# Zeroing of buffers taken off GpSimd and given to VectorE and ScalarE, with the instruction order planned anew

## The chip, the cores and the metric

The kernel runs on one core of one Trainium2 chip. The metric is device time in microseconds (us) of one execution; each kernel is executed several times and the median counts. The engines of the core that matter here are TensorE (PE, matrix products into PSUM), VectorE (DVE), ScalarE (ACT), GpSimd (POOL, which here also issues all loads) and SyncE (SP, which issues the stores). Each engine works through its own queue in order; semaphores tie the queues together.

## The reference

Two steps are fused: attention within a symmetric window of 32 positions to either side, and a mixture of eight low-rank adapters of which each token uses two. Cut to what matters:

```python
# q, k, v: (8, 8, 576, 64) float32
scores = (1 / np.sqrt(64)) * np.matmul(q, k.transpose(0, 1, 3, 2))
mask = np.abs(pos[:, None] - pos[None, :]) <= 32
scores = np.where(mask, scores, -1e9)
attn = softmax(scores, axis=-1)
x = (attn @ v).transpose(0, 2, 1, 3).reshape(4608, 512)
...
logits = x @ w_gate                      # w_gate: (512, 8)
topk = the 2 largest logits of each row
w = softmax over these two
delta = sum over the two of w * ((x @ A[e]) @ B[e])   # A[e]: (512, 16), B[e]: (16, 512)
return x + delta
```

## The kernel before

**Tiling.** The eight batches are worked one behind another in a pipeline. Two heads are worked as a pair, so a batch has four pairs; a pair is a unit u (32 in all). Of a batch, q and k each come in three tiles of 96 partitions (LD, line 275), cast from float32 to float16 by the transfer; v comes in two halves (LV, line 280) of one load for four heads each. All loads stand in GpSimd's queue, in one order; the compiled program lets eight of them be in flight, the next waits for the landing of the one eight places before it. There are seven raw buffers `l` for q and for k, three buffers `vbd` for v, two `qT` and two `kT`, four `PT`.

**Steps of the attention.** RG (line 290) regroups a raw tile on VectorE into `c`, called a cast below, three buffers deep. TR (298) transposes it on TensorE into PSUM (two slots T). EQ (304) and EK (312, two instructions, one for each half of the partitions) copy it on ScalarE into `qT` and `kT`. SV (285) moves the odd positions of a v half to other partitions on VectorE. SC (318 and 324) makes a tile of masked scores of eight key blocks in PSUM (three slots W); EX (329) takes the exponential on ScalarE into `PT`; there are 36 such tiles, 4.5 for a batch. PV (342) multiplies with v, and a column of ones in `vbd` gives the sum; MU (351 and 352) is the normalisation on VectorE, one for each unit, into `x`.

**Steps of the adapters, once for each batch.** TX (364) transposes `x`, XE (370) copies it out of PSUM on VectorE, PZ (378) makes logits and low-rank products, G1, GA and G2 (395 to 416) find the two adapters and their weights, TZ and ZE (423, 427) transpose the result, PD (433 and 436) adds x and delta in PSUM, OB (445 on ScalarE, 447 on VectorE) copies it out, ST (453) stores it from SyncE.

**What must be zeroed or set to one.** `kT` holds two heads block-diagonally, so 64x64 corners must be zero; `vbd` holds two heads side by side, so the other head's columns must be zero and one column must be one; the margins of `PT` and of `qT` must be zero. These places are written once and never overwritten. Before, VectorE did it for buffer 0 of each kind and for all four `PT`, ahead of everything else (lines 476 to 489 by way of 500 to 505). GpSimd did it for `vbd` 1, `kT` and `qT` 1 and `vbd` 2 at three fixed places in its load queue: behind the eighth and the tenth load, and behind the sixteenth, after the six transfers of the weights (491 to 497, called from 516 to 518).

**What sets the order.** `tasks()` lists all steps with an engine, a cost in us, what they depend on, and a due time: the unit they belong to plus an offset for each kind from `OFF`. `plan()` is a list scheduler: at each step it takes, for the engine that can start something earliest, the startable step with the earliest due time, and appends it to the order; it keeps count of PSUM slots and of one transfer stream. The instructions are then issued in that order, so each engine's queue follows it. The zeroing was not among the steps; the start times of the engines in `plan()` stood for it.

## Time and profile before

| | before |
|---|---|
| median of 3 runs | 161.4 us (160.46 to 161.6) |
| profiled execution | 158.86 us |
| its span, first to last instruction | 156.9 us |
| TensorE busy | 123.2 us (79%) |
| VectorE busy | 119.8 us (76%) |
| ScalarE busy | 113.1 us (72%) |
| GpSimd busy | 67.1 us (43%) |
| mean granted TensorE clock | 0.954 |

"Span" is from the first to the last instruction of the profiled execution; the execution's own time is a little longer. A row of a timeline gives the start, the duration, the engine, the line of the kernel, the operation with its output and input, and in brackets how long the engine had been idle before and what it waited for. Rows of one line that follow each other are merged (x4), and their duration is then from the first start to the last end. Rows of groups give the count, the total busy time and the mean duration of one in ns. A load on GpSimd's timeline is the time that GpSimd takes to issue it, not the transfer.

### The profile page before, as it was taken

Reading aid. Unit: us, or ns where it says so; the run is one execution under the profiler, and the core shown is the slowest. Engines: PE = TensorE matmul, PEld = TensorE weight load, DVE = VectorE, ACT = ScalarE, POOL = GpSimd, SP = SyncE. Lnnn points to the kernel's source line nnn. Section 1 sums busy time; section 2 is a strip of 40 time slices with the busy share of each in tenths; the row PEclk is TensorE's granted clock in tenths of the full one; section 3 lists DMA queues with packets and bytes.
Section 4 is the critical chain, followed back from the end, with each engine's and each line's share of the span. In section 5 each row is a group of like instructions: output and inputs, shape, how many; then the busy total and the mean of one; then the engine's idle time right before and its main releaser. Section 6 shows DMA issues by size and latency. Waiting matters only on the chain.

```text
span 156.9 us, 4220 instructions
## 1 busy us (share of the span) xinstructions
PE 123.2 (79%) x1720; PEld 103.7 (66%) x1720; DVE 119.8 (76%) x273; ACT 113.1 (72%) x141; POOL 67.1 (43%) x91
## 2 busy tenths in 40 slices
PE   0024998659988998998699989979999899893480
PEld 0013767449967896797579778967798689672250
DVE  6799928996798879996976989779688967955310
ACT  0306799944499999969898998897998992743150
POOL 7999999899848555354553407000000000000000
PEclk9999999975899999999999999999999999999659
DMA  2999569938999999999999999992420350077125
GB/s 31 150 172 113 85 97 174 122 31 115 157 188 202 190 242 203 178 260 209 183 207 234 276 200 204 142 253 63 164 87 4 106 192 7 6 280 263 61 87 214
DMA packets 38771, 24.13 MB, mean 154 GB/s; under 512 B 24800, under 2 KB 34144, under 8 KB 38752
## 3 DMA queue, kind: packets, MB, share of 16 engines
q0 software_dynamic: 33504, 14.43, 80.5%
q1 hardware_dynamic: 5248, 9.44, 17.4%
q8 instruction: 13, 0.21, 0.6%
q14 instruction: 6, 0.05, 0.1%
HBM read 28.85 MB, written 9.44 MB: 244 GB/s over the span
## 4 chain that ended last, share of the span: by engine, by line
PE 39%; DVE 18%; POOL 16%; DMA 10%; ACT 7%; issue 7%; SPq 0%; POOLq 0%; ACTq 0%; DVEq 0%
PE W L342 6%; PE W L324 5%; PE W L318 5%; DVE x L352 5%; PE W L433 5%; POOL l L275 5%; PE W L436 5%; PE T L364 4%; DMA vbd<-in_v_dram 4%; PE T L298 4%; DMA l<-in_k_dram 3%; POOL vbd L482 3%; DVE zs L416 3%; ACT kT L312 2%; PE W L378 2%
## 5 line engine op out<-in xcount | busy, mean ns | idle before, releaser
L329 ACT ACTIVATE PT<-W 128x1024 f16<-128x1024 f32 x36 | 36.2, 1028 | 6.7 <-PE W L324 6.1
L312 ACT COPY kT<-T 64x768 f16<-64x768 f16 x48 | 38.1, 794 | 3.2 <-PE T L298 2.7
L298 PE MATMUL T<-ident,c 96*128 96x96 f16 x384 | 25.1, 216 | 17.5 <-DVE c L290 15.9
L298 PEld LDWEIGHTS <-c 96*128 96x128 f16 x384 | 20.8, 104 | 18.6 <-DVE c L290 16.8
L290 DVE COPY c<-l 96x1024 f16<-96x1024 f16 x48 | 30.4, 654 | 2.1 <-DMA l<-in_q_dram 1.3
L342 PE MATMUL W<-vbd,PT 128*128 128x130 f16 x416 | 29.9, 225 | 0.8 <-ACT PT L329 0.6
L352 DVE TENSOR_TENSOR x<-W,rc 128x640 f16<-128x640 f32 x32 | 26.4, 824 | 1.2
L342 PEld LDWEIGHTS <-PT 128*128 128x128 f16 x416 | 26.4, 100 | 1.3 <-issue 1.3
L304 ACT COPY qT<-T 128x768 f16<-128x768 f16 x24 | 19.1, 800 | 10.8 <-PE T L298 10.6
L324 PEld LDWEIGHTS <-kT 128*128 128x128 f16 x288 | 19.4, 99 | 9.5 <-issue 1.0
L324 PE MATMUL W<-qT,kT 128*128 128x128 f16 x288 | 22.4, 222 | 0.2 <-ACT kT L312 0.2
L280 POOL DMA_DIRECT2D vbd<-in_v_dram x16 | 14.0, 878 | 19.5 <-DMA vbd<-in_v_dram 7.3
L318 PE MATMUL W<-ident,mask 128*128 128x512 f16 x72 | 22.2, 391 | 0.2 <-DVE x L352 0.2
L445 ACT COPY ob<-W 128x1024 f32<-128x1024 f32 x16 | 16.2, 1015 | 6.8 <-PE W L436 4.4
L370 DVE COPY xT<-T 128x1024 f16<-128x1024 f16 (+1 forms) x24 | 13.7, 598 | 8.2 <-PE T L364 7.8
L275 POOL DMA_DIRECT2D l<-in_k_dram x24 | 16.4, 684 | 6.5 <-DMA l<-in_k_dram 2.8
L433 PE MATMUL W<-B_sb,zT 128*128 128x512 f16 x40 | 16.4, 410 | 3.2 <-DVE x L352 2.4
L436 PEld LDWEIGHTS <-xT 128*128 128x128 f16 x160 | 13.3, 104 | 8.3 <-issue 4.1
L275 POOL DMA_DIRECT2D l<-in_q_dram x24 | 15.7, 653 | 2.9 <-issue 1.2
L436 PE MATMUL W<-ident,xT 128*128 128x128 f16 x160 | 16.7, 231 | 0.0
L285 DVE COPY vbd<-vbd 32x2304 f16<-32x2304 f16 x16 | 13.9, 868 | 0.5
L364 PE MATMUL T<-ident,x 128*128 128x128 f16 x160 | 13.1, 231 | 0.1
(55 smaller groups left out, 121.1 us busy)
## 6 DMA issues: line engine op xcount, KB each, us to landing
out_dram<-ob SPq DMA_DIRECT2D x24, 256.0 KB, 2.5
l<-in_q_dram POOLq DMA_DIRECT2D x24, 192.0 KB, 9.3
l<-in_k_dram POOLq DMA_DIRECT2D x24, 192.0 KB, 9.5
vbd<-in_v_dram POOLq DMA_DIRECT2D x16, 288.0 KB, 9.4
out_dram<-ob SPq DMA_DIRECT2D x16, 192.0 KB, 2.8
WA_sb<-in_moe_A_dram POOLq DMA_DIRECT2D x4, 32.0 KB, 7.5
B_sb<-in_moe_B_dram POOLq DMA_DIRECT2D x1, 128.0 KB, 4.4
WA_sb<-in_moe_w_gate_dram POOLq DMA_DIRECT2D x1, 8.0 KB, 5.3
```

Of the source, the lines that this page charges most:

```text
L275: keep(nc.gpsimd.dma_start(out=raw[w][(NT3 * b + t) % NRAW], in_=src[FT * t:FT * t + FT]))
L290: keep(nc.vector.tensor_copy(out=cst[w][i % NCAST], in_=raw[w][i % NRAW].rearrange("p o (j d) -> p j o d", j=J)))
L298: keep(nc.tensor.matmul(out=tp[:, FT * slot:FT * slot + FT], lhsT=src[:, j, :], rhs=ident[0:FT, 0:FT], is_transpose=True, start=True, stop ...
L312: keep(nc.scalar.copy(out=dst.rearrange("p a (r f j) -> p a r f j", r=2, j=4), in_=kt[64 * o:64 * o + 64]))
L318: keep(nc.tensor.matmul(out=p[:, i:i + 4], lhsT=maskT, rhs=bcast(ident, 1, 4), start=True, stop=False))
L324: keep(nc.tensor.matmul(out=p[:, i], lhsT=kTs[b % 2][:, NB * n + a, :], rhs=qTs[b % 2][:, c0:c0 + 128], start=False, stop=(i % 4 == 3)))
L329: keep(nc.scalar.activation(out=PTs[T % NPT][:, :, 64:192], in_=ps("SC", T).rearrange("p (i c) -> p i c", c=128), func=AF.Exp, scale=1.0 / ...
L342: keep(nc.tensor.matmul(out=po[:, GS * g:GS * g + 2 * VD], lhsT=PTs[T % NPT][:, sl, off:off + 128], rhs=rhs[:, :, V0 - 1:V0 + D], start=(i ...
L352: keep(nc.vector.tensor_tensor(out=xs[b % NX].rearrange("p g (h n d) -> p g h n d", h=2, n=NP)[:, :, :, n], in0=pog[:, :, :, 1:VD], in1=bc ...
L364: keep(nc.tensor.matmul(out=tp[:, c0:c0 + 128], lhsT=xs[b % NX][:, g, 128 * c:128 * c + 128], rhs=ident, is_transpose=True, start=True, st ...
L433: keep(nc.tensor.matmul(out=pd[:, i], lhsT=zTs[b % 2][:, g], rhs=B_sb, start=True, stop=False))
L436: keep(nc.tensor.matmul(out=pd[:, i, 128 * c:128 * c + 128], lhsT=xTs[b % NXT][:, g, c], rhs=ident, start=False, stop=(c == 3)))
```

## The change

The zeroing becomes steps of the schedule. ZK (buffers `kT` and `qT`), ZV (`vbd`) and ZP (`PT`) get a cost and a due time like all others, and the steps that need the zeroed places depend on them. ZK and ZP, and ZV of `vbd` 0 and 2, are VectorE memsets; ZV of `vbd` 1 is done on ScalarE by copying from a small zeroed tile whose 66 columns are repeated 36 times. No memset is left on GpSimd except those of the identity and the mask. All offsets in `OFF` are new; the costs of some steps are lower (a q or k load 1.15 instead of 1.25, a v load 1.8 instead of 2.95, a store 0.5 instead of 0.75 for each part, SV 0.78 instead of 0.95) and one higher (G1 1.08 instead of 0.95); the engines' start times in `plan()` and its horizon differ. So the order of the instructions on every engine differs throughout. The order of the loads among themselves, and the place of the weights behind the sixteenth load, are the same, and no computing step is added or left out.

On VectorE the queue now begins with a memset of the small zero tile and one of a piece of `qT` 0; ZK of both buffers and the two columns of ones of `vbd` 1 follow, then the first cast. ZP of the four `PT` stand between the first four casts, ZV of `vbd` 0 and 2 between the following casts and shifts. On ScalarE the two copies of ZV stand first.

```diff
@@ -55,9 +55,10 @@
         self.take, self.give, self.lat = take, give, lat
 
 
-OFF = {"LD": -10.1, "LV": -8.3, "RG": -7.2, "TR": -11.5, "EQ": 11.0, "EK": -0.6, "SV": 23.8, "SC": -1.9,
-       "EX": 19.8, "PV": -0.9, "MU": -1.8, "TX": -16.6, "XE": -2.6, "PZ": 4.4, "G1": -3.0, "GA": 2.0,
-       "G2": 15.0, "TZ": 1.1, "ZE": -13.8, "PD": 9.7, "OB": 7.2}
+OFF = {"LD": -10.16, "LV": -7.58, "RG": -2.51, "TR": -3.5, "EQ": -0.91, "EK": 8.24, "SV": 11.71,
+       "SC": -2.02, "EX": 9.98, "PV": -0.24, "MU": -0.5, "TX": 0.38, "XE": -20.72, "PZ": 4.91,
+       "G1": -40.48, "GA": 17.51, "G2": -27.59, "TZ": -20.47, "ZE": 17.82, "PD": 10.1, "OB": -2.95,
+       "ZK": -28.38, "ZV": 29.47, "ZP": 16.04}
 
 
 def tasks(off=OFF):
@@ -69,6 +70,15 @@
         t.due = u + off[key[0]]
         t.seq = len(ts)
         ts[key] = t
+
+    for i in range(2):
+        for o in (0, 1):
+            add(("ZK", i, o), -4.0 + 8 * i, "DVE", 1.05, [])
+    for i in range(NPT):
+        add(("ZP", i), -3.0 + i, "DVE", 0.56, [])
+    for i in range(NV):
+        for o in (0, 1):
+            add(("ZV", i, o), 4 * i, "ACT" if i == 1 else "DVE", 2.2 if i == 1 else 1.2, [])
 
     def tiles_of(b):
         return range(NS * b // TB, (NS * b + NS - 1) // TB + 1)
@@ -79,10 +89,10 @@
             for t in range(NT3):
                 for w in (0, 1):
                     i = NT3 * b + t - NRAW
-                    add(("LD", b, w, t), u0 + 1.333 * t, "DMA", 1.25,
+                    add(("LD", b, w, t), u0 + 1.333 * t, "DMA", 1.15,
                         [("RG", i // NT3, w, i % NT3)], lat=2.0)
             for o in (0, 1):
-                add(("LV", b, o), u0 + o, "DMA", 2.95,
+                add(("LV", b, o), u0 + o, "DMA", 1.8,
                     [("PV", NP * (b - NV) + n) for n in range(NP)], lat=2.0)
             for t in range(NT3):
                 u = u0 + 1.333 * t
@@ -98,7 +108,7 @@
                 add(("EK", b, t), u, "ACT", 1.60, [("TR", b, 1, t)] + old,
                     give=("TR", b, 1, t))
             for o in (0, 1):
-                add(("SV", b, o), u0, "DVE", 0.95, [("LV", b, o)])
+                add(("SV", b, o), u0, "DVE", 0.78, [("LV", b, o)])
 
         for T in range(NT):
             last = TB * T + TB - 1
@@ -111,6 +121,7 @@
                     need |= {("EQ", bb, s // BT), ("EK", bb, s // BT)}
                     if s % NB != NB - 1:
                         need.add(("EQ", bb, (s + 1) // BT))
+                    need |= {("ZK", bb % 2, 0), ("ZK", bb % 2, 1)}
             u = (TB * T) / NB
             add(("SC", T), u, "PE", 0.90, list(need), take="W")
             pold = [("PV", v) for v in range(NU)
@@ -122,7 +133,9 @@
             bb = u // NP
             add(("PV", u), u, "PE", 0.80,
                 [("EX", T) for T in range(NB * u // TB, (NB * u + NB - 1) // TB + 1)]
-                + [("SV", bb, 0), ("SV", bb, 1)], take="W")
+                + [("ZP", T % NPT) for T in range(NB * u // TB, (NB * u + NB - 1) // TB + 1)]
+                + [("SV", bb, 0), ("SV", bb, 1), ("ZV", bb % NV, 0), ("ZV", bb % NV, 1)],
+                take="W")
             add(("MU", u), u, "DVE", 1.05,
                 [("PV", u)] + [("TX", bb - NX, h) for h in range(3)], give=("PV", u))
             if u % NP != NP - 1:
@@ -136,7 +149,7 @@
                     [("TX", bb, h)] + [("PD", bb - NXT, i) for i in range(3)],
                     give=("TX", bb, h))
             add(("PZ", bb), v0, "PE", 1.2, [("XE", bb, h) for h in range(3)], take="W")
-            add(("G1", bb), v0, "DVE", 0.95, [("PZ", bb)])
+            add(("G1", bb), v0, "DVE", 1.08, [("PZ", bb)])
             add(("GA", bb), v0, "ACT", 0.22, [("G1", bb)])
             add(("G2", bb), v0, "DVE", 1.95, [("GA", bb)], give=("PZ", bb))
             add(("TZ", bb), v0, "PE", 0.30, [("G2", bb)], take="T")
@@ -149,11 +162,11 @@
                     1.02 if n == 2 else 0.70, [("PD", bb, h), ("ST", k // 3, k % 3)],
                     give=("PD", bb, h))
                 off["ST"] = off["OB"]
-                add(("ST", bb, h), v0 + 0.8 * h, "DMO", 0.75 * n, [("OB", bb, h)], lat=2.0)
+                add(("ST", bb, h), v0 + 0.8 * h, "DMO", 0.5 * n, [("OB", bb, h)], lat=2.0)
     return ts
 
 
-def plan(off=OFF, horizon=0.0):
+def plan(off=OFF, horizon=0.036):
 
     ts = tasks(off)
     for t in ts.values():
@@ -164,7 +177,7 @@
         for d in t.deps:
             d.users.append(t)
     free = {e: 0.0 for e in ("PE", "ACT", "DVE", "DMA", "DMO")}
-    free["DMA"], free["DVE"], free["PE"], free["ACT"] = 1.5, 8.5, 9.0, 4.0
+    free["DMA"], free["DVE"], free["PE"], free["ACT"] = 1.5, 1.1, 4.5, 3.0
     slots = {"W": [0.0] * NW, "T": [0.0] * NTP}
     wait = {e: [t for t in ts.values() if t.eng == e and t.left == 0] for e in free}
     order, dma_free = [], 1.5
@@ -472,21 +485,29 @@
                                 base=64, channel_multiplier=-1,
                                 pattern=[[0, 2], [1, 2], [2, 32]]))
 
-    def init_kq(i, eng):
-        keep(eng.memset(kTs[i][0:64, :, 64:128], 0.0))
-        keep(eng.memset(kTs[i][64:128, :, 0:64], 0.0))
-        keep(eng.memset(qTs[i][:, 0:QP], 0.0))
-        keep(eng.memset(qTs[i][:, QP + NP * S:], 0.0))
-
-    def init_v(i, eng):
-        keep(eng.memset(vbd[i][0:64, :, VW + V0 - 2:VW + V0 + D], 0.0))
-        keep(eng.memset(vbd[i][64:128, :, V0 - 2:V0 + D], 0.0))
-        keep(eng.memset(vbd[i][0:64, :, V0 - 1:V0], 1.0))
-        keep(eng.memset(vbd[i][64:128, :, VW + V0 - 1:VW + V0], 1.0))
-
-    def init_p(i, eng):
-        keep(eng.memset(PTs[i][:, :, 0:64], 0.0))
-        keep(eng.memset(PTs[i][:, :, 192:256], 0.0))
+    zero = const.tile([128, D + 2], F16, name="zero")
+
+    def ZK(i, o):
+        keep(nc.vector.memset(kTs[i][64 * o:64 * o + 64, :, 64 - 64 * o:128 - 64 * o], 0.0))
+        if o == 0:
+            keep(nc.vector.memset(qTs[i][:, 0:QP], 0.0))
+            keep(nc.vector.memset(qTs[i][:, QP + NP * S:], 0.0))
+
+    def ZV(i, o):
+        c0 = V0 + VW * (1 - o)
+        dst = vbd[i][64 * o:64 * o + 64, :, c0 - 2:c0 + D]
+        if i == 1:
+            keep(nc.scalar.copy(out=dst, in_=bcast(zero[64 * o:64 * o + 64], 1, NS)))
+        else:
+            keep(nc.vector.memset(dst, 0.0))
+        c1 = V0 + VW * o
+        keep(nc.vector.memset(vbd[i][64 * o:64 * o + 64, :, c1 - 1:c1], 1.0))
+
+    def ZP(i):
+        keep(nc.vector.memset(PTs[i][:, :, 0:64], 0.0))
+        keep(nc.vector.memset(PTs[i][:, :, 192:256], 0.0))
+
+    do.update(ZK=ZK, ZV=ZV, ZP=ZP)
 
     def weights():
         for c in range(4):
@@ -496,26 +517,17 @@
                             in_=moe_w_gate.rearrange("(c p) e -> p c e", p=128)))
         keep(nc.gpsimd.dma_start(out=B_sb, in_=moe_B.rearrange("e r d -> (e r) d")))
 
+    keep(nc.vector.memset(zero, 0.0))
+    keep(nc.vector.memset(qTs[0][:, QP + S:QP + S + 32], 0.0))
     loads = 0
-    init_kq(0, nc.vector)
-    init_p(0, nc.vector)
-    keep(nc.vector.memset(qTs[0][:, QP + S * 1:QP + S * 1 + 32], 0.0))
-    init_v(0, nc.vector)
-    for i in range(1, NPT):
-        init_p(i, nc.vector)
     for t in order:
         do[t.key[0]](*t.key[1:])
         if t.key[0] in ("LD", "LV"):
             loads += 1
             if loads == 4:
                 constants()
-            elif loads == 8:
-                init_v(1, nc.gpsimd)
-            elif loads == 10:
-                init_kq(1, nc.gpsimd)
             elif loads == 16:
                 weights()
-                init_v(2, nc.gpsimd)
 
     for p in (small, psum, const):
         p.release()
```

## The prediction

> **What bounds the kernel now.** I read the page's slices first, to find where the engines are starved, then the timelines of GpSimd, VectorE and ScalarE over the first 45 us, and last a table by stretches for the transfer rate. The slices show two things: the transfers have a hole at the fourth to sixth slice and one at the ninth (a slice is 3.92 us), and the granted TensorE clock falls just behind the second.
>
> ```profile
> PEclk9999999975899999999999999999999999999659
> DMA  2999569938999999999999999992420350077125
> ```
>
> The GpSimd timeline shows what stands in the load queue at those places. Each row below is the first memset of a group, or the load that follows the group.
>
> ```profile
> 8.28 2.10 POOL L482 MEMSET vbd<- 64x2376 f16 x1
> ...
> 13.26 0.78 POOL L275 DMA_DIRECT2D l<-in_q_dram  x1
> ...
> 14.87 2.23 POOL L476 MEMSET kT<- 64x2304 f16 x1
> ...
> 19.63 0.63 POOL L275 DMA_DIRECT2D l<-in_q_dram  x1
> ...
> 29.75 2.12 POOL L482 MEMSET vbd<- 64x2376 f16 x1
> ...
> 34.75 0.65 POOL L275 DMA_DIRECT2D l<-in_q_dram  x1
> ```
>
> Start to start, the groups hold the queue for 13.26 - 8.28 = 5.0, 19.63 - 14.87 = 4.8 and 34.75 - 29.75 = 5.0 us, 14.8 in all. No load can be issued in that time. The stretches show the price (columns: stretch, its length, busy time of PE, weight loads, DVE, ACT and POOL, granted clock, DMA share, GB/s):
>
> ```profile
> 8.00:14.00 6.00, 1.80 (x21) 1.59 (x22) 5.96 (x9) 0.92 (x2) 5.89 (x6) 1.00 1.40 168
> 14.00:18.00 4.00, 2.96 (x27) 2.27 (x26) 3.94 (x4) 3.84 (x5) 3.92 (x4) 1.00 0.72 105
> 18.00:21.00 3.00, 3.00 (x34) 2.33 (x32) 2.79 (x3) 2.29 (x3) 2.94 (x6) 1.00 0.02 1
> 22.00:29.00 7.00, 6.18 (x98) 5.37 (x99) 4.81 (x10) 6.95 (x9) 6.50 (x8) 1.00 1.43 178
> 29.00:32.00 3.00, 1.14 (x15) 0.73 (x12) 3.00 (x1) 2.21 (x3) 2.96 (x4) 1.00 4.97 98
> 32.00:37.00 5.00, 3.70 (x45) 3.28 (x46) 4.63 (x6) 3.31 (x4) 4.92 (x7) 0.64 0.29 19
> 37.00:42.00 5.00, 5.00 (x60) 4.76 (x59) 3.28 (x8) 0.59 (x1) 5.00 (x8) 0.68 1.18 162
> 42.00:54.00 12.00, 11.03 (x165) 9.17 (x163) 10.79 (x29) 11.77 (x17) 7.33 (x10) 1.00 1.45 191
> 54.00:80.00 26.00, 23.31 (x365) 20.16 (x363) 22.27 (x59) 23.33 (x32) 12.27 (x17) 1.00 1.43 210
> 80.00:105.00 25.00, 24.11 (x371) 20.93 (x370) 19.87 (x51) 23.04 (x29) 7.70 (x12) 1.00 1.25 220
> ```
>
> Well supplied, loads move 162 to 191 GB/s. Against 178, the stretch 14 to 18 loses 4 x (1 - 105/178) = 1.6 us, 18 to 21 loses 3.0 and 32 to 37 loses 5 x (1 - 19/178) = 4.5: 9.1 us of dead stream. The stretch 29 to 32 is the weights, with their small pieces; they stay, and cost 3 us of the stream.
>
> The same memsets also slow VectorE. Its timeline in the first 40 us:
>
> ```profile
> 1.05 1.02 DVE L476 MEMSET kT<- 64x1152 uint32 x1 [1.05 <-PEq L536]
> ...
> 4.27 1.05 DVE L482 MEMSET vbd<- 64x1188 uint32 x1 [0.19 <-issue]
> ...
> 6.81 0.09 DVE L484 MEMSET vbd<- 64x36 f16 x1 [0.16 <-issue]
> ```
>
> ```profile
> 8.81 1.85 DVE L290 COPY c<-l 96x1024 f16<-96x1024 f16 x1
> ```
>
> ```profile
> 8.81 5.10 DVE L290 COPY c<-l 96x1024 f16<-96x1024 f16 x4
> ...
> 17.41 2.54 DVE L285 COPY vbd<-vbd 32x2304 f16<-32x2304 f16 x1
> ```
>
> ```profile
> 28.17 0.75 DVE L285 COPY vbd<-vbd 32x2304 f16<-32x2304 f16 x1
> 28.95 5.50 DVE L290 COPY c<-l 96x1024 f16<-96x1024 f16 x2
> ...
> 38.28 0.42 DVE L290 COPY c<-l 96x1024 f16<-96x1024 f16 x1 [1.06 <-DMA l<-in_q_dram]
> ```
>
> A cast takes 0.42 us and a half-shift of v (L285) 0.75 when GpSimd does no memset. Beside the memsets the first cast takes 1.85, the four from 8.81 take 5.10 in place of 1.7, the shift 2.54, the two from 28.95 take 5.50 in place of 0.8. That is 3.4 + 1.8 + 4.7 = 9.9 us of VectorE time, all in front of TensorE's transposes. ScalarE shows the result:
>
> ```profile
> 4.17 1.28 ACT L304 ACT_TABLE_LOAD   x1 [4.17 <-DVE qT L502]
> 11.57 0.80 ACT L304 COPY qT<-T 128x768 f16<-128x768 f16 x1 [6.12 <-PE T L298]
> ```
>
> ```profile
> 41.41 1.02 ACT L329 ACTIVATE PT<-W 128x1024 f16<-128x1024 f32 x1 [4.44 <-PE W L324]
> ```
>
> It starts its first copy at 11.57, and the eighth exponential (EX 7), which needs only the first two batches, is over only at 42.4. From 54 to 105 TensorE is busy 23.31 of 26 and 24.11 of 25 us: there it is the limit, and the loads stay ahead.
>
> **The change, part by part.** *GpSimd's memsets go.* The 14.8 us leave the load queue. The ninth load follows the eighth at once, then the loads are limited by the transfers (eight can be in flight, by the program's semaphores). The stream ends 9.1 us earlier if nothing else holds it.
>
> *VectorE's head.* In the new order twelve memsets stand before the first cast: four of 64x1152 (kT, both buffers) at 1.02 plus a 0.19 gap, and eight small ones at about 0.1. So the first cast starts at 1.05 + 4 x 1.21 + 0.8 = 6.7, not 8.81, and takes 0.42, not 1.85. From the end of the first cast before (10.66) to the first copy on ScalarE (11.57) it is 0.91 us, so this copy starts at 6.7 + 0.42 + 0.91 = 8.0. The memsets of PT and of vbd 0 and 2 stand between the casts now. What VectorE gains in work is two kT parts (2.04), two vbd parts (2.1) and seven small ones (0.6), 4.7 us; what it sheds is the 9.9 us of slowed copies. Net it is relieved in the head.
>
> *ScalarE zeroes vbd 1* by two copies of 2376 elements. No such copy is in the trace; the nearest rows are the copy of 768 elements at 0.80 and the exponential of 1024 at 1.03, 0.9 ns for each further element. My estimate is 0.80 + 1608 x 0.0009 = 2.2 us each. Behind the table load (1.28, from about 1.2, since its writer is now VectorE's first memset) they end at 7.0, and ScalarE's first real work is at 8.0, so they cost nothing. If the repeated source doubled them they would end at 11.4 and delay the first copy by 3.4.
>
> *ScalarE's chain to EX 7.*
>
> ```profile
> L329 ACT ACTIVATE PT<-W 128x1024 f16<-128x1024 f32 x36 | 36.2, 1028 | 6.7 <-PE W L324 6.1
> L312 ACT COPY kT<-T 64x768 f16<-64x768 f16 x48 | 38.1, 794 | 3.2 <-PE T L298 2.7
> ```
>
> The new order has 6 copies of q, 12 halves of k and 8 exponentials up to there: 6 x 0.80 + 12 x 0.794 + 8 x 1.028 = 22.6 us. From 8.0 the chain ends at 30.6; before it ended at 42.4: 11.8 us earlier. The loads must hold with it.
>
> ```profile
> l<-in_q_dram POOLq DMA_DIRECT2D x24, 192.0 KB, 9.3
> ...
> vbd<-in_v_dram POOLq DMA_DIRECT2D x16, 288.0 KB, 9.4
> ```
>
> A q or k tile is 0.197 MB, a v half 0.295, a batch 1.77. Batch 0 is in at about 14 (168 GB/s in 8 to 14). At 178 GB/s the seven transfers up to batch 1's last k (1.475 MB) are in at 14 + 8.3 = 22.3; ScalarE wants it at 8.0 + 5 x 0.80 + 10 x 0.794 + 5 x 1.028 = 25.1. Batch 2's first pair is in at 14 + 9.9 + 3 (weights) + 2.2 = 29.1, its second at 31.3. ScalarE itself wants the first only at 30.6, so both fit.
>
> *The order planned anew.* The new VectorE order puts the casts of a batch earlier. Batch 2's first three casts stand ahead of normalisation 4 and of the copies of batch 0's transposes, which free the PSUM for EX 7's scores; so VectorE blocks until 31.3 there, and behind that come the third cast, normalisation 4 with its reciprocal (1.0) and a copy or two (0.7 each) before those scores: EX 7 ends near 34 to 35, not 30.6. That is a gain of 8 there. Further on, the last cast of batch 4 follows normalisation 11 (before: 13), that of batch 7 follows normalisation 23 (before: 26). VectorE works in order, so a late load now holds up normalisation 12 or 24, and with it TensorE, which waits for their PSUM.
>
> ```profile
> 68.58 0.20 DVE L351 RECIPROCAL rc<-W 128x10 f32<-128x10 f32 x1
> ```
>
> ```profile
> 115.86 0.22 DVE L351 RECIPROCAL rc<-W 128x10 f32<-128x10 f32 x1 [0.57 <-PE W L342]
> ```
>
> ```profile
> q1 hardware_dynamic: 5248, 9.44, 17.4%
> ```
>
> These are normalisations 12 and 24. Shifted by 10 us they come at 58.6 and 105.9. Stores take 17.4% of 156.9 us, 3.4 us of the stream for each batch. Batch 4's last k needs 6.78 MB behind the first eight loads: at 191 GB/s 35.5 us, with weights (3) and about half a batch of stores (2) it is in at 54.5. Batch 7's last k needs 12.09 MB: 63.3 us, with weights and three batches of stores (10.2) at 90.5. So the loads keep ahead of both. For the rest of the new order, ScalarE's and TensorE's included, the trace has no price. Its bounds are the 4.6 us that TensorE idles between 42 and 105 (0.97 + 2.69 + 0.89), if a better order fills them, and as much the other way; I take zero, the middle, because the same instructions run there on the same three nearly full engines. The last batch's chain from normalisation 31 to the last store has no step less or more: zero, within 1 us.
>
> *Sum.* ScalarE's chain alone would give 11.8, the stream gives 9.1, the block at batch 2 leaves 8 at EX 7. As the loads have 4 us in hand at batch 4, part of that block can be made good (TensorE stood at half clock at this point before); I take 10, between the stream and the chain: span 156.9 - 10 = 146.9. The profiled execution took 158.86 us, 1.96 over its span, so 148.9 for such an execution. The median of the runs shown, 161.4, lies 2.54 above it; on that scale it is 151.4 us.
>
> **A rule that speaks against it.** GpSimd now issues its loads while VectorE copies at full speed.
>
> ```profile
> 47.93 1.11 POOL L275 DMA_DIRECT2D l<-in_k_dram  x1 [0.47 <-DVE c L290]
> ...
> 96.46 0.83 POOL L280 DMA_DIRECT2D vbd<-in_v_dram  x1
> ```
>
> The first issue overlaps a VectorE copy and takes 1.11 us, where one of the same kind takes 0.65 at 34.75: 0.46 more. Even if each of 64 loads paid that, 29 us would be spread over the 95 up to the last issue, in which the queue mostly waits for landings, so I price it at nothing. The Trainium skill (SBUF — State Buffer, section "SBUF: two separate sides") warns that descriptors of transfers issued from GpSimd cannot be written while VectorE runs a copy in a two-port mode. Its measured case has an issue of about 620 ns grow to about 3100; by that 64 loads would need 198 us and the kernel would be slower than before. The trace shows the direction and a fifth of the size.
>
> **The rivals.** *More gain:* the new order also fills TensorE's 4.6 us of idle time: 151.4 - 4.6 = 146.8. For it speaks that VectorE's casts stand earlier, against it that TensorE is at 96% from 80 to 105 already.
>
> *The loads become the bound:* if they run at 162 GB/s, as from 37 to 42, batch 4's last k takes 41.9 us and is in at 60.9, and normalisation 12, behind the last cast, comes at 61.3, 7.3 us earlier than before, not 10: 161.4 - 7.3 = 154.1.
>
> *Slower, through the casts that stand ahead:* VectorE blocks at batch 7's last cast, behind normalisation 23, and normalisation 24 comes later than 115.9. That takes 14 + 3 + 10.2 + L over 115.5, so L over 88.3 us for 12.09 MB, under 137 GB/s. At 130 GB/s it is 93 us, normalisation 24 at 120.6, the time 161.4 + 4.7 = 166. No stretch with a full queue is that slow.
>
> *Slower, through issues locked out by VectorE's copies:* the last load before was issued at 96.46; it would have to come after that again, so 70 issues would have to take over 1.37 us each. The row above has 1.11.
>
> *The change does little:* the memsets were hidden, and another limit holds the head. The holes in the stream and the clock of 0.64 behind them speak against it: 161.
>
> **How the numbers follow.** Forecast 0.50 (148.5 to 153); more gain 0.20 (145 to 148.5); loads bound 0.15 (153 to 158); little 0.05; the two slower ones 0.07 and 0.03. Changes under 1% cannot be told from none here; that is 159.8 to 163.0. So faster 0.85, same 0.05, slower 0.10. The range reaches from the second case's lower end to the third's upper end, 145 to 158, and leaves out the last three cases and the edges.
>
> **What would show it.** GpSimd's rows should hold loads back to back up to the weights, and the slices no hole in the transfers before 35 us; the first 12 casts should take 0.42 each, and the v shifts 0.75; ScalarE's first copy should start near 8 and EX 7 end near 34; the granted clock should not fall to 0.5 near 35. Normalisations 12 and 24 should come near 59 and 106. I am wrong if VectorE's rows show casts ended by a wait for a load, several us each, after 45 us, if a GpSimd issue takes 1.5 us or more in the middle, or if ScalarE's zeroing copies end after 8 us.

## The result and the profile after

| | before | after |
|---|---|---|
| median (lowest to highest) | 160.93 us (160.29 to 161.6) | 150.15 us (147.73 to 151.74) |
| profiled execution | 158.86 us | 148.89 us |
| its span | 156.9 us | 146.7 us |
| TensorE, VectorE, ScalarE, GpSimd busy | 123.2, 119.8, 113.1, 67.1 us | 119.8, 113.3, 116.3, 51.9 us |
| mean granted TensorE clock | 0.954 | 0.979 |

The changed kernel takes 0.9215 of the time before, with an interval of 0.9116 to 0.9315; the kernel before was run again beside it. Two later comparisons with the same two kernels gave 0.9307 [0.9247, 0.9368] and 0.9447 [0.9374, 0.9521]. That is a gain of 8.9 to 12.6 us. The ratios and their intervals leave out executions that took over 1.5% longer than the fastest of the same kernel; the medians take all. Effects of a us or two are as small as the scatter between comparisons, so each experiment below is set against the changed kernel of its own comparison where there is one.

First the slices of after, in the same two rows as before: granted clock and DMA share, 40 slices of 3.67 us.

```profile
PEclk9999999999999999999999999999999999999686
DMA  2999999999999999999999959990542023058035
```

Both holes in the transfers are gone, and the clock falls only in the tail. The table by stretches of after has the columns of the prediction's (stretch, length, PE, weight loads, DVE, ACT, POOL, granted clock, DMA share, GB/s):

```profile
8.00:14.00 6.00, 5.02 (x43) 3.70 (x44) 5.06 (x13) 5.56 (x8) 4.52 (x7) 1.00 1.40 164
14.00:18.00 4.00, 3.15 (x42) 2.40 (x41) 3.45 (x7) 3.67 (x6) 2.55 (x4) 1.00 1.30 197
18.00:21.00 3.00, 2.14 (x35) 1.73 (x33) 2.67 (x6) 2.32 (x3) 2.41 (x3) 1.00 1.54 196
...
32.00:37.00 5.00, 4.88 (x85) 4.52 (x83) 4.56 (x11) 3.94 (x5) 2.60 (x4) 1.00 1.46 174
...
54.00:80.00 26.00, 23.96 (x359) 20.46 (x357) 22.16 (x52) 22.90 (x30) 11.10 (x16) 1.00 1.36 225
80.00:105.00 25.00, 24.59 (x379) 21.39 (x377) 22.56 (x61) 23.60 (x32) 3.27 (x4) 1.00 0.87 160
```

The stretch 18 to 21 moved 1 GB/s and now moves 196; 32 to 37 moved 19 and now moves 174. TensorE, which did 1.80 us of work in the first of these stretches, does 5.02. The timeline of VectorE in after shows the casts (now line 303), the v shifts (298) and the normalisations (364):

```profile
6.43 0.42 DVE L303 COPY c<-l 96x1024 f16<-96x1024 f16 x1
...
28.71 0.42 DVE L303 COPY c<-l 96x1024 f16<-96x1024 f16 x1 [1.50 <-DMA l<-in_q_dram]
29.67 0.47 DVE L303 COPY c<-l 96x1024 f16<-96x1024 f16 x1 [0.54 <-DMA l<-in_k_dram]
...
31.12 0.47 DVE L303 COPY c<-l 96x1024 f16<-96x1024 f16 x1 [0.38 <-DMA l<-in_q_dram]
31.51 0.20 DVE L364 RECIPROCAL rc<-W 128x10 f32<-128x10 f32 x1
...
59.47 0.20 DVE L364 RECIPROCAL rc<-W 128x10 f32<-128x10 f32 x1
...
63.55 0.76 DVE L303 COPY c<-l 96x1024 f16<-96x1024 f16 x2 [0.35 <-PE T L311]
...
104.38 0.22 DVE L364 RECIPROCAL rc<-W 128x10 f32<-128x10 f32 x1 [0.67 <-PE W L355]
```

The first cast takes 0.42 us where it took 1.85. The rows at 28.71, 29.67 and 31.12 are the forecast block at batch 2: VectorE waits there for loads, and normalisation 4 (31.51) comes behind. The groups of instructions show the same over all 48 casts, and what it does to TensorE's transposes. First the groups of before (count, busy time, mean ns of one, idle time ahead of them and what ended it), then of after:

```profile
L290 DVE COPY c<-l 96x1024 f16<-96x1024 f16 x48 | 30.4, 654 | 2.1 <-DMA l<-in_q_dram 1.3 <-DMA l<-in_k_dram 0.5
...
L298 PE MATMUL T<-ident,c 96*128 96x96 f16 x384 | 25.1, 216 | 17.5 <-DVE c L290 15.9 <-ACT kT L312 1.6
```

```profile
L311 PE MATMUL T<-ident,c 96*128 96x96 f16 x384 | 24.0, 213 | 9.9 <-DVE c L303 8.0 <-ACT kT L325 0.9 <-ACT qT L317 0.3
...
L303 DVE COPY c<-l 96x1024 f16<-96x1024 f16 x48 | 20.3, 450 | 3.3 <-DMA l<-in_q_dram 2.3 <-DMA l<-in_k_dram 0.5 <-PE T L311 0.4
```

A cast takes 450 ns in the mean instead of 654, and TensorE's wait for casts ahead of its transposes falls from 15.9 to 8.0 us.

The timeline of ScalarE has the two zeroing copies, the first copy of work, and EX 7:

```profile
2.04 4.36 ACT L500 COPY vbd<-zero 64x2376 f16<-64x2376 f16 x2
7.78 0.80 ACT L317 COPY qT<-T 128x768 f16<-128x768 f16 x1 [1.38 <-PE T L311]
...
32.59 1.02 ACT L342 ACTIVATE PT<-W 128x1024 f16<-128x1024 f32 x1 [1.99 <-PE W L337]
```

The zeroing ends at 6.40, 1.38 us ahead of the first copy, as that row's wait says. Last the load queue on GpSimd's timeline:

```profile
71.81 0.82 POOL L293 DMA_DIRECT2D vbd<-in_v_dram  x1 [8.50 <-PE W L355]
...
86.47 0.82 POOL L293 DMA_DIRECT2D vbd<-in_v_dram  x1 [8.99 <-PE W L355]
...
88.63 1.11 POOL L293 DMA_DIRECT2D vbd<-in_v_dram  x1
```

The queue has become so early that it stands still for 8.5 and 9.0 us, because all three `vbd` buffers are still being read. The loads are ahead of their users, not behind.

**Where the time went.** The normalisations are one for each unit, and always in the same order; their start times measure how far the kernel has come. (Each number is the start of a reciprocal's row, as the three above; the last column is the span. c1 and c2 are the changed kernel again, in later comparisons; the numbers in brackets are those of the experiments below.)

| kernel | no. 0 | no. 4 | no. 7 | no. 12 | no. 31 | end |
|---|---|---|---|---|---|---|
| before | 24.02 | 38.62 | 50.03 | 68.58 | 136.26 | 156.9 |
| after | 19.43 | 31.51 | 40.63 | 59.47 | 127.51 | 146.7 |
| c1 | 20.64 | 32.75 | 41.68 | 60.91 | 129.08 | 148.1 |
| c2 | 19.80 | 32.33 | 41.72 | 60.82 | 129.31 | 148.5 |
| zero_moved (1) | 23.05 | 36.42 | 47.16 | 65.49 | 133.20 | 154.3 |
| order_only (2) | 23.53 | 41.47 | 51.05 | 69.12 | 137.66 | 157.0 |
| weights_later (3) | 19.51 | 29.33 | 39.78 | 59.59 | 126.94 | 146.0 |
| zero_placed (4) | 26.81 | 36.79 | 47.28 | 66.18 | 133.90 | 154.8 |
| old_lengths (5) | 19.97 | 31.44 | 40.48 | 59.05 | 129.12 | 148.4 |
| no_scalar (6) | 21.74 | 32.74 | 41.69 | 60.80 | 129.41 | 148.7 |
| zero_as_new (7) | 21.36 | 31.22 | 41.84 | 60.89 | 128.70 | 149.6 |
| later memsets alone (9) | 19.73 | 32.40 | 42.68 | 60.61 | 138.44 | 156.6 |
| earlier memsets alone (10) | 19.54 | 32.56 | 41.38 | 58.98 | 129.34 | 148.1 |

From normalisation 12 to 31 the kernel before takes 67.7 us and the changed one 68.0. So of the 10.2 us of span, 9.1 are won before normalisation 12, 0.4 are lost between, and 1.4 are won behind normalisation 31 (20.6 against 19.2 us). What is left to settle is which part of the change won the 9.1: the empty load queue, the faster copies, the places of the zeroing, or the order of the other steps.

### The profile page after: what moved, and what is told of

It reads as the page before. It is cut to its first block, busy times and chain, and to the rows that moved or that the text cites. A ratio compares the mean times of both kernels' runs of the same rounds, so it can differ in the third digit from the quotient of the medians.

```text
span 146.7 us, 4230 instructions
## 1 busy us (share of the span) xinstructions
PE 119.8 (82%) x1720; PEld 100.8 (69%) x1720; DVE 113.3 (77%) x284; ACT 116.3 (79%) x143; POOL 51.9 (35%) x79
## 4 chain that ended last, share of the span: by engine, by line
PE 38%; DMA 21%; ACT 15%; DVE 11%; issue 6%; POOL 5%; SPq 0%; ACTq 0%; POOLq 0%; DVEq 0%
DMA vbd<-in_v_dram 12%; PE W L355 6%; ACT kT L325 5%; PE W L331 5%; DMA l<-in_q_dram 5%; ACT PT L342 5%; PE W L337 5%; PE W L446 5%; PE W L449 5%; DMA out_dram<-ob 4%; PE T L377 4%; PE W L391 4%; POOL l L288 3%; PE T L311 3%; ACT qT L317 3%
## 5 line engine op out<-in xcount | busy, mean ns | idle before, releaser
L342 ACT ACTIVATE PT<-W 128x1024 f16<-128x1024 f32 x36 | 36.9, 1025 | 6.3 <-PE W L337 5.4
L311 PE MATMUL T<-ident,c 96*128 96x96 f16 x384 | 24.0, 213 | 9.9 <-DVE c L303 8.0
L355 PE MATMUL W<-vbd,PT 128*128 128x130 f16 x416 | 29.1, 219 | 1.7 <-DVE vbd L298 0.8
L311 PEld LDWEIGHTS <-c 96*128 96x128 f16 x384 | 20.0, 101 | 11.7 <-DVE c L303 9.6
L355 PEld LDWEIGHTS <-PT 128*128 128x128 f16 x416 | 25.2, 97 | 2.2 <-issue 2.2
L303 DVE COPY c<-l 96x1024 f16<-96x1024 f16 x48 | 20.3, 450 | 3.3 <-DMA l<-in_q_dram 2.3
L293 POOL DMA_DIRECT2D vbd<-in_v_dram x16 | 13.5, 846 | 25.5 <-PE W L355 17.5
L288 POOL DMA_DIRECT2D l<-in_k_dram x24 | 15.8, 658 | 6.0 <-DVE rc L364 2.6
L377 PE MATMUL T<-ident,x 128*128 128x128 f16 x160 | 12.2, 219 | 2.3 <-DVE xT L383 1.8
L298 DVE COPY vbd<-vbd 32x2304 f16<-32x2304 f16 x16 | 12.3, 767 | 1.6 <-DMA vbd<-in_v_dram 1.2
(46 smaller groups left out, 113.1 us busy)
```

The costliest lines, as they stand in the source:

```text
L288: keep(nc.gpsimd.dma_start(out=raw[w][(NT3 * b + t) % NRAW], in_=src[FT * t:FT * t + FT]))
L303: keep(nc.vector.tensor_copy(out=cst[w][i % NCAST], in_=raw[w][i % NRAW].rearrange("p o (j d) -> p j o d", j=J)))
L311: keep(nc.tensor.matmul(out=tp[:, FT * slot:FT * slot + FT], lhsT=src[:, j, :], rhs=ident[0:FT, 0:FT], is_transpose=True, start=True, stop ...
L342: keep(nc.scalar.activation(out=PTs[T % NPT][:, :, 64:192], in_=ps("SC", T).rearrange("p (i c) -> p i c", c=128), func=AF.Exp, scale=1.0 / ...
L355: keep(nc.tensor.matmul(out=po[:, GS * g:GS * g + 2 * VD], lhsT=PTs[T % NPT][:, sl, off:off + 128], rhs=rhs[:, :, V0 - 1:V0 + D], start=(i ...
```

## The experiments

The changed kernel itself went along in two of the three comparisons, as their yardstick (c1 and c2).

> The changed kernel itself, for comparison on the same chip as the other three. Both theories: ratio to the kernel before 0.91 to 0.94, as measured already.

> The changed kernel once more, for comparison on the same chip: a ratio of 0.92 to 0.94.

Measured: 149.35 us, 0.9307 [0.9247, 0.9368], and 151.34 us, 0.9447 [0.9374, 0.9521].

**1. The kernel before, with only the engine of three groups changed.** Nothing of the order changes; the memsets that GpSimd did are issued at the same places on VectorE.

```diff
             elif loads == 8:
-                init_v(1, nc.gpsimd)
+                init_v(1, nc.vector)
             elif loads == 10:
-                init_kq(1, nc.gpsimd)
+                init_kq(1, nc.vector)
             elif loads == 16:
                 weights()
-                init_v(2, nc.gpsimd)
+                init_v(2, nc.vector)
```

> The kernel before with its old order of all steps; only the three groups of GpSimd memsets are issued on VectorE, at the same places of the program. Theory A (the gain comes from the load queue and from VectorE's copies that the memsets slowed): the transfer holes at 14 to 21 and 32 to 37 us close, casts take 0.42, and the time is 151 to 154, a ratio of 0.94 to 0.96; the old order starts its first cast at 8.8, 2 us later than the new one. Theory B (the newly planned order brings the gain): 158 to 161, a ratio of 0.98 to 1.00.

Measured: 156.89 us, 0.9706 [0.9626, 0.9786] of the kernel before, where the changed kernel on the same chip has 0.9307. The table by stretches of this kernel says that the holes are closed:

```profile
18.00:21.00 3.00, 3.00 (x19) 1.96 (x18) 2.18 (x6) 2.96 (x5) 2.27 (x3) 1.00 1.48 194
...
32.00:37.00 5.00, 4.50 (x60) 4.24 (x58) 3.38 (x7) 3.09 (x4) 3.26 (x5) 0.69 1.51 195
```

So 194 and 195 GB/s, where after has 196 and 174, and yet less than half of the gain; and the granted clock in the second stretch is 0.69. VectorE's timeline, and then TensorE's, show what holds it at batch 1:

```profile
27.84 1.05 DVE L482 MEMSET vbd<- 64x1188 uint32 x1 [0.28 <-issue]
...
30.75 0.78 DVE L290 COPY c<-l 96x1024 f16<-96x1024 f16 x2
```

```profile
31.23 0.51 PE L298 MATMUL T<-ident,c 96*128 96x96 f16 x8 [2.61 <-DVE c L290]
```

The memsets of `vbd` 2 stand in a lump ahead of two casts, and TensorE waits 2.61 us for the first of these. The casts themselves take 0.4 us each. Behind this wait comes the granted clock of 0.69, where after has 1.00, so part of what is missing is TensorE's clock; how much, these rows do not separate. A full load stream and unslowed copies are therefore not enough for the whole gain while memsets stand in a lump ahead of a cast that TensorE waits for.

**2. The changed kernel, with the three groups put back on GpSimd.** ZK of buffers 1 and ZV of `vbd` 1 and 2 are issued in GpSimd's queue behind the eighth, tenth and sixteenth load, as in the kernel before; all else keeps the new order.

```diff
...
+            elif loads == 8:
+                for o in (0, 1):
+                    ZV(1, o, nc.gpsimd)
+            elif loads == 10:
+                for o in (0, 1):
+                    ZK(1, o, nc.gpsimd)
             elif loads == 16:
                 weights()
+                for o in (0, 1):
+                    ZV(2, o, nc.gpsimd)
```

> The changed kernel with the new order of all steps, but the memsets of vbd 1, kT and qT 1 and vbd 2 stand on GpSimd again, at the three old places of the load queue. Theory A: the holes in the transfers come back and the time is 158 to 163, a ratio of 0.98 to 1.01; casts that stand earlier in VectorE's queue wait for loads, so it may be slower than the kernel before. Theory B: 150 to 154, a ratio of 0.93 to 0.96.

Measured: 159.53 us, 0.9943 [0.9909, 0.9978]. Of this kernel, first the stretches, then a row of the waits over the first 50 us (total, count and longest in us):

```profile
18.00:21.00 3.00, 3.00 (x23) 2.10 (x21) 2.71 (x5) 1.85 (x3) 3.00 (x4) 1.00 0.11 6
...
32.00:37.00 5.00, 2.76 (x39) 2.23 (x40) 1.84 (x4) 2.95 (x4) 4.96 (x7) 0.97 0.51 29
```

```profile
DVE c L303 <- DMA l<-in_q_dram: 7.2, 4, 4.5
```

The holes are back, and the early casts of the new order stand in VectorE's queue waiting for loads that come late: 7.2 us. Normalisation 4 comes at 41.47, 2.9 us later than in the kernel before. This is the mechanism of the prediction's rival of casts that stand ahead, though at batch 2 and not at batch 7: with the memsets left where they were, the new order has nearly nothing to give.

**3. The changed kernel, with the weights four loads later.** This takes the block at batch 2 away: the small transfers of the weights no longer lie ahead of batch 2's first loads.

```diff
-            elif loads == 16:
+            elif loads == 20:
```

> The changed kernel with the six weight transfers behind the 20th load instead of the 16th, so that batch 2's first two pairs of tiles come ahead of them. Theory A1 (the block of VectorE at batch 2's first casts costs time to the end): the casts start near 26 instead of 28.7 and 31.1, EX 7 at 30 to 31 instead of 32.6, and the time is 2 us below the changed kernel's. Theory A2 (TensorE makes good what the block costs, or the low-rank product waits for the weights instead): within 1 us of the changed kernel.

Measured: 149.1 us (147.16 to 151.58), against 149.35 (148.28 to 151.62) of the changed kernel beside it; the runs scatter too much for an interval. In VectorE's timeline normalisation 4 comes at 29.33, and a v shift then waits for its load:

```profile
29.33 0.20 DVE L364 RECIPROCAL rc<-W 128x10 f32<-128x10 f32 x1
...
34.31 0.75 DVE L298 COPY vbd<-vbd 32x2304 f16<-32x2304 f16 x1 [1.55 <-DMA vbd<-in_v_dram]
```

Counted from normalisation 0, normalisation 4 comes after 9.8 us (after and c1: 12.1), normalisation 7 after 20.3 (21.2 and 21.0) and normalisation 12 after 40.1 (40.0 and 40.3): what was won is gone again by batch 3. So by these traces the block at batch 2 costs the changed kernel nothing at its end; the weights only moved the wait to other loads. The times alone do not settle it: the two lowest, 147.16 and 148.02, lie below all four of the changed kernel beside them, so a us or so is not excluded.

**4. The old order, the zeroing on VectorE at places chosen by hand.** As experiment 1, but the margins of `PT` and `vbd` 0 are zeroed behind the seventh load step and `vbd` 2 behind the thirteenth, so that fewer memsets stand before the first cast.

```diff
-    init_p(0, nc.vector)
...
-    init_v(0, nc.vector)
-    for i in range(1, NPT):
-        init_p(i, nc.vector)
...
+            elif loads == 7:
+                for i in range(NPT):
+                    init_p(i, nc.vector)
+                init_v(0, nc.vector)
+            elif loads == 13:
+                init_v(2, nc.vector)
```

> The kernel before, with its old order of all other steps; all zeroing is on VectorE and placed by hand: kT and qT 0 first, the four first casts right behind, then PT and vbd 0, vbd 1, kT and qT 1 as before between the next casts, and vbd 2 in front of normalisation 0, where VectorE stood idle for 2.7 us. The zeroing alone at its old places gave 157 us. Theory A (what is still missing is the place of the memsets in VectorE's queue: 2 us late first cast, and 3 us of vbd 2's memsets in front of batch 1's last casts): 150 to 153, a ratio of 0.93 to 0.95, normalisation 12 near 61. Theory B (the order of the other steps brings the rest): 155 to 157, a ratio of 0.965 to 0.98, normalisation 12 near 64 to 65.

Measured: 158.14 us, 0.9844 [0.9739, 0.9949], no better than experiment 1 (the two intervals overlap). VectorE's timeline of it, and TensorE's:

```profile
4.83 0.50 DVE L290 COPY c<-l 96x1024 f16<-96x1024 f16 x1 [1.30 <-DMA l<-in_q_dram]
...
18.73 0.76 DVE L290 COPY c<-l 96x1024 f16<-96x1024 f16 x2
```

```profile
19.21 1.46 PE L298 MATMUL T<-ident,c 96*128 96x96 f16 x16 [7.11 <-DVE c L290]
```

The first cast starts 4 us earlier than before, but now the postponed memsets stand in one lump ahead of batch 0's third pair of casts, and TensorE waits 7.11 us for these. I had placed them badly. For the question that it was made for, stream or copies, the run says nothing; it says that the place within VectorE's queue is worth several us.

**5. The changed kernel with the old transfer lengths in the planner** (q and k loads 1.25, v loads 2.95, stores 0.75 for each part), all else as new.

```diff
-                    add(("LD", b, w, t), u0 + 1.333 * t, "DMA", 1.15,
+                    add(("LD", b, w, t), u0 + 1.333 * t, "DMA", 1.25,
...
-                add(("LV", b, o), u0 + o, "DMA", 1.8,
+                add(("LV", b, o), u0 + o, "DMA", 2.95,
...
-                add(("ST", bb, h), v0 + 0.8 * h, "DMO", 0.5 * n, [("OB", bb, h)], lat=2.0)
+                add(("ST", bb, h), v0 + 0.8 * h, "DMO", 0.75 * n, [("OB", bb, h)], lat=2.0)
```

> The changed kernel, planned with the old transfer lengths (1.25 for q and k, 2.95 for v, 0.75 for a store's part) and the new offsets and other costs; the zeroing stays scheduled. Casts and normalisations change places from batch 0 on. Theory A (the zeroing off the load queue and its places bring the gain): 149 to 152. Theory B (the shorter lengths matter, because the order fits the true landings): 153 to 157.

Measured: 150.7 us, 0.9404 [0.9339, 0.9469], which lies between the changed kernel's own three ratios; normalisation 12 at 59.05. The shorter lengths in the planner win nothing that can be measured.

**6. The changed kernel with `vbd` 1 zeroed on VectorE**, in the place in VectorE's order that the two columns of ones had, ahead of the first cast.

```diff
-            nc.scalar.copy(out=dst, in_=bcast(zero[64 * o:64 * o + 64], 1, NS))
+            nc.vector.memset(dst, 0.0)
```

> The changed kernel with vbd 1 zeroed by two VectorE memsets at the same place of the order, in front of the first cast, instead of the two ScalarE copies. Theory A (the head is carried to the end): the first cast starts 2.4 us later, at 8.9, and the time is 1.5 to 2.5 us longer than the changed kernel's. Theory B (batch 2's landings bind the head anyway): within 1 us of the changed kernel's.

Measured: 150.5 us (147.76 to 153.24), too scattered for an interval, and between the changed kernel's medians (149.35 to 151.34). VectorE's timeline has the first cast 2.5 us later:

```profile
8.92 0.42 DVE L303 COPY c<-l 96x1024 f16<-96x1024 f16 x1
```

Normalisation 0 is then at 21.74, normalisation 7 at 41.69 and normalisation 12 at 60.80 (c2: 19.80, 41.72 and 60.82). The 2 us are made up by normalisation 7, and as far as these runs can tell ScalarE's part in the zeroing is not needed for the gain.

**7. The old order of all other steps, the zeroing exactly where the changed kernel has it.** The offsets, costs and lengths are those of the kernel before. ZK of both buffers and ZV of `vbd` 1 (on ScalarE) come first; the rest stands behind single casts, as in the new order of VectorE.

```diff
...
+    behind = {("RG", 0, 0, 0): [(ZP, 0)], ("RG", 0, 1, 0): [(ZP, 1)], ("RG", 0, 0, 1): [(ZP, 2)],
+              ("RG", 0, 1, 1): [(ZP, 3), (ZV, 0, 0)], ("RG", 0, 0, 2): [(ZV, 0, 1)],
+              ("RG", 0, 1, 2): [(ZV, 2, 0)], ("RG", 1, 0, 0): [(ZV, 2, 1)]}
...
     for t in order:
         do[t.key[0]](*t.key[1:])
+        for f, *arg in behind.get(t.key, []):
+            f(*arg)
```

> The old order of all other steps, but the zeroing stands exactly where the changed kernel has it: vbd 1 on ScalarE, kT and qT in front of the first cast, PT, vbd 0 and vbd 2 between the same casts and shifts. Theory A (the place of the zeroing in the queues is what the two earlier trials lacked): 150 to 152, a ratio of 0.93 to 0.945, normalisation 4 near 32 and 12 near 60 to 61. Theory B (the new order of the other steps in the first 35 us is needed too): 153 to 156, a ratio of 0.955 to 0.97, normalisation 4 near 34 to 36.

Measured: 152.15 us, 0.9511 [0.9458, 0.9564], beside 151.34 and 0.9447 [0.9374, 0.9521] of the changed kernel in the same comparison. Its timelines, VectorE's and then ScalarE's:

```profile
6.44 0.64 DVE L290 COPY c<-l 96x1024 f16<-96x1024 f16 x1
...
31.22 0.21 DVE L351 RECIPROCAL rc<-W 128x10 f32<-128x10 f32 x1
```

```profile
33.73 1.02 ACT L329 ACTIVATE PT<-W 128x1024 f16<-128x1024 f32 x1 [2.60 <-PE W L324]
```

First cast at 6.44 (after: 6.43), EX 7 at 33.73 (after: 32.59), normalisation 12 at 60.89 (c2: 60.82). In these two executions all of what is won before normalisation 12 comes without the new order of the other steps. Only behind normalisation 31 does the old order take 20.9 us where the new one takes 19.2; the two ratios' intervals overlap, so that difference is seen in the spans and not in the times.

**8 to 10. Four GpSimd memsets of no use, put into the changed kernel in the middle**, where loads are far ahead: they write a buffer that nobody reads. At first at two places (behind the 52nd and the 60th load), then at one of them alone.

```diff
+    idle = const.tile([64, NS, D + 2], F16, name="idle")
...
+            elif loads in (52, 60):
+                for _ in range(4):
+                    keep(nc.gpsimd.memset(idle, 0.0))
```

> The changed kernel with eight more GpSimd memsets of an unused tile (64 x 2376), four each in the two stretches in which GpSimd waits 8.5 and 9 us for a buffer, so that they delay no load by more than a fraction of a us; about 17 us of memsets. Theory A1 (slowed VectorE copies cost time to the end by themselves): the casts and v shifts beside them take 1.3 to 3.2 us instead of 0.4 to 0.75, and the time is 3 to 6 us longer than the changed kernel's. Theory A2 (the copies are slowed but there is room for it in this stage, the harm in the kernel before came from the held-up loads): at most 1.5 us longer.

> The changed kernel with only the second group of four unused GpSimd memsets, in the wait of 9 us near 77 to 86, where VectorE has casts and v shifts beside them and no load is held up. Theory A1 (slowed copies alone cost time to the end, as much as VectorE loses or more): four or five copies take 1.4 to 2.6 us, 5 to 6 us more in all, and the time is 5 to 8 us longer than the changed kernel's. Theory A2 (the loss came from held-up loads or a disturbed chip): at most 1.5 us longer.

> The changed kernel with only the first group, in the wait of 8.5 us near 63 to 72, where VectorE runs no cast and no v shift, or at most the two casts at its beginning. Theory A1: within 1.5 us of the changed kernel's. If GpSimd memsets cost by themselves, without copies beside them: 3 us or more longer.

Measured: both places 157.76 us, 0.982 [0.9736, 0.9903]; only the later place (60) 157.78, 0.9743 [0.9663, 0.9823]; only the earlier (52) 150.6, 0.9435 [0.9368, 0.9502], with the changed kernel at 151.34 and 0.9447 beside the last two. Of the kernel with the later place alone, GpSimd's timeline and then VectorE's:

```profile
80.53 9.32 POOL L532 MEMSET idle<- 64x2376 f16 x4
96.21 0.82 POOL L293 DMA_DIRECT2D vbd<-in_v_dram  x1 [6.36 <-PE W L355]
```

```profile
81.50 1.74 DVE L298 COPY vbd<-vbd 32x2304 f16<-32x2304 f16 x1
83.27 0.42 DVE L383 COPY xT<-T 128x512 f16<-128x512 f16 x1
83.73 1.81 DVE L303 COPY c<-l 96x1024 f16<-96x1024 f16 x1
...
86.44 1.40 DVE L303 COPY c<-l 96x1024 f16<-96x1024 f16 x1
87.86 2.59 DVE L298 COPY vbd<-vbd 32x2304 f16<-32x2304 f16 x1
```

The queue held no load up: behind the memsets GpSimd still waits 6.36 us for a buffer. But the two shifts and two casts take 1.74 + 1.81 + 1.40 + 2.59 = 7.54 us in place of 2 x 0.75 + 2 x 0.42 = 2.3, that is 5.2 more. Normalisation 15 to 19 takes 20.9 us (75.10 to 96.01) where c2 takes 14.85 (73.35 to 88.20), 6.1 more; with both places it takes 21.7 (74.89 to 96.55). By the ratios the whole kernel takes 4.7 us longer than the changed one (0.9743 and 0.9447 of 160.22), as an estimate with both intervals 3 to 6.5. How VectorE's delay reaches TensorE, a row of TensorE's timeline and one of the stretches of this kernel show:

```profile
92.63 1.01 PE L331 MATMUL W<-ident,mask 128*128 128x512 f16 x2 [4.34 <-DVE x L365]
```

```profile
93.00:96.00 3.00, 3.00 (x27) 2.71 (x26) 1.62 (x5) 2.92 (x4) 0.00 (x0) 0.50 0.00 0
```

TensorE waits 4.34 us for a normalisation, and behind this wait its granted clock is 0.50, where c2 has 1.00. As an estimate this clock takes another 3 x 0.5 = 1.5 us of TensorE's work up to 96. Now the kernel with the earlier place alone, the same two timelines:

```profile
63.45 8.82 POOL L532 MEMSET idle<- 64x2376 f16 x4
```

```profile
63.08 5.04 DVE L303 COPY c<-l 96x1024 f16<-96x1024 f16 x2 [0.35 <-PE T L311]
...
71.20 1.09 DVE L424 TENSOR_SCALAR s<-dm 128x5 f32<-128x5 f32 x1
```

Two casts take 5.04 us where after's row at 63.55 has 0.76, and an instruction of five elements takes 1.09 instead of 0.17: 4.3 + 0.9 = 5.2 us more of VectorE here too, and no loss that the times show. Normalisation 15 comes at 73.84 where c2 has 73.35, and normalisation 19 at 88.23 where c2 has 88.20. But this execution was ahead before the memsets, with normalisation 12 at 58.98 where c2 has 60.82; from 12 to 19 it takes 29.25 us and c2 27.38, 1.9 more. In after VectorE waits for TensorE at this place (the 0.35 of the row at 63.55, and 0.39, 1.24 and 0.46 us ahead of three later instructions up to 68.59, 2.4 in all), and there part of the delay is taken up; in the kernel with the earlier place TensorE's granted clock stays at 1.00 from 60 to 75. So copies that are slowed by GpSimd's memsets alone, with no load held up, can cost the whole kernel about 4.7 us, or less than the scatter of the times (some 2 us by the trace), for the same 5.2 us.

The profiled execution of the later place took 158.74 us, 1 us above that kernel's median, and lost 2.0 us against c2 between normalisations 12 and 15, ahead of the memsets (14.49 and 12.53); so the lengths of stretches within it are used, not its span.

## Why the prediction was right

**The path and the sum.** The forecast was a span of 146.9 us and 148.9 for such an execution; it was 146.7 and 148.89. That it hit so closely is luck: the spans of the four executions run from 145.9 to 149.8. The median was put at 151.4 and came out at 150.15, 1.25 lower: the 2.54 us by which the median shown before lay above its profiled execution were only 1.26 after.

**The head.** First cast 6.7, measured 6.43; ScalarE's zeroing 2.2 us each, measured 2.18 (4.36 for two); first copy 8.0, measured 7.78; batch 2's first pair 29.1 and second 31.3, and VectorE's waits end at 28.71 and 29.67 for the first pair's two tiles and at 31.12 for the second pair's first; EX 7 over at 34 to 35, measured 33.61. The estimate for an operation that the trace didn't have, ScalarE's copy of a repeated source, held; its cost for each further element was taken from two rows of the same engine. The zeroing ended at 6.40 and not 7.0 because the table load began at 0.74, before VectorE's first memset (0.82), and not behind it. The 9.9 us of slowed copies leave out a pair of casts in the row at 14.72 of before (2.66 us in place of 0.8); with it they are 11.7. The sum used neither.

**The 9.1 and the 10.** The term "10, between the stream and the chain" was 9.1 at normalisation 12, and the term "zero, within 1 us" for the last batch was 1.4. The two errors cancel. The 1.4 belongs to the new order of the other steps, since the old order has 20.9 us there in experiment 7 too; what in that order brings it wasn't tried. The middle's zero was right from end to end (67.7 and 68.0 us), and the rival of more gain didn't occur. It was not zero all along: normalisation 24 was forecast at 105.9 and came at 104.38, 11.5 us earlier than before, and 2.7 of that were lost again by normalisation 31.

**What was right only in part is the sentence that the stream gives 9.1.** Experiment 1 closes the holes and unslows the copies and wins 4.7 us (0.0294 of 160.66), and experiment 4, with the same engines and other places, 2.5, which the intervals do not tell apart. Experiment 7 with the new places wins 7.8, the changed kernel beside it 8.9. The dead stream is a condition and not a price: where it is filled, the next thing that is late is the cast behind a lump of memsets, and the gain depends on how many of those stand ahead of TensorE's next input (experiments 1 and 7 differ in nothing but the zeroing: its places, and `vbd` 1 on ScalarE). In experiment 1 TensorE's granted clock is 0.69 from 32 to 37, in experiment 7 it is 1.00; the clock's share of the difference was not separated. The prediction did count the new places, in VectorE's head and in ScalarE's chain, and so came to the right size.

**The block at batch 2** was forecast to leave 8 us at EX 7 (8.8 came) and to be made good in part. By experiment 3's traces it is made good in full.

**Loads as the bound, and the slower rivals.** After 45 us no cast waits for a load; the queue instead waits 8.5 and 9.0 us for buffers. The rival that the casts standing ahead make it slower showed only where GpSimd kept its memsets (experiment 2, at batch 2), and did not even there make it slower than before. The last load was issued at 88.63, ahead of the 96.46 of before. Its issue took 1.11 us, beside a v shift (88.54), the longest behind 30 us. The prediction took 1.11 for the longest of before too; there one takes 1.40 (72.83, beside a shift at 73.03), just over the 1.37 that the rival needed of every issue. But in the mean an issue of the 64 loads took 0.72 us before and 0.71 after (46.1 and 45.5 us busy): VectorE's faster copies did not slow the issues. The Trainium skill (SBUF — State Buffer, section "SBUF: two separate sides") has a transfer issued from GpSimd take about 3100 ns beside a VectorE copy, and the prediction took this for the issue and worked 198 us out of it. The same section of the Trainium skill says that such a transfer is blocked until VectorE's instruction ends, plus about 115 ns; as an estimate that allows no more than 0.82 + 0.75 + 0.12 = 1.7 us here (a v load's issue and a shift), and the 1.40 and the 1.11 lie within it. So the 3100 was the wrong figure to carry over to copies this short.

**What stays open.** How the gain in the head divides between the load stream and the unslowed copies was not separated: no run has GpSimd's memsets beside the head's casts without also holding up loads. Experiments 8 to 10 price the slowed copies in the middle only. Nor was it separated which of the new places counts, the shorter head or the memsets set singly between casts.

## What to carry to other kernels

A memset on GpSimd can cost twice: it holds back the loads queued behind it, and it stretches VectorE's copies beside it. Moving it to VectorE closes both, but the place decides: in lumps ahead of the casts that TensorE waits for it gave less than half of the gain; with a shorter head, one part on ScalarE and the rest spread singly between the casts it gave nearly all. Before pricing a slowed or added instruction, look whether its engine has idle time behind it, and how long TensorE would wait: the same 5.2 us cost about 4.7 us in one place, where TensorE then waited 4.34 us at a stretch and its clock fell, and no time clear of the scatter eight loads earlier.

## What the runs showed of the hardware

How a VectorE instruction fares beside a GpSimd memset of 2.1 to 2.3 us goes by its kind, not by its size. Copies from SBUF to SBUF in float16 wait (experiments 8 to 10: 0.42 becomes 1.40 and 1.81, 0.75 becomes 1.74 and 2.59; the two of 0.76 in all become 5.04), and so does the operation of a tensor of five elements with a scalar (0.17 becomes 1.09). A copy out of PSUM between two of these does not (83.27 above: 0.42), nor do operations on two tensors (0.17 to 0.20 us each from 69.2 to 71.3, beside the memsets of experiment 10, as without memsets). The Trainium skill (SBUF — State Buffer, section "Who interferes with whom") lets copies, casts and the operation of a tensor with a scalar be blocked by GpSimd for the length of its instruction; the rows agree, in that each of these is longer by no more than the 2.1 to 2.3 us of one memset.
